# k weights in three row chunks, x tile 1 behind b1 on the scalar queue, filler matmuls between the first transposes, last tile stored in two column parts

## Chip, cores, metric

One core of a Trainium2 chip. The metric is the device time of one execution in microseconds (us). Most executions of one kernel agree within a few tenths of a us; where a run is more than 1.5% above the fastest of the same kernel it is called slow and is not compared. The profile's engines are PE (matmul), PEld (weight load), DVE, ACT, POOL and SP; "q" behind a name means the engine's sequencer, which issues DMAs.

## The reference, cut to what matters

```python
x = A_x                               # (1, 2048, 448), bfloat16
xn = _layernorm(x, axis=-1)
s = _A_ref(xn, A_wqkv, A_wo)          # linear attention, 16 heads of 28, feature map elu-like
g = _silu(_B_ref(xn, B_w1, B_b1, B_w2, B_b2))   # squared-relu MLP, hidden size 1792
return x + s * g
```

Everything begins with the layer norm of x. x is 16 tiles of 128 tokens; "x tile 1" is the second one. "k" are the attention's keys, b1 is the first bias of the MLP, and H is the MLP's hidden layer. Its first four blocks are computed in two halves: the first for the tokens of tiles 0 and 1, the second for those of tiles 2 and 3. When the second halves start, the slow start of the kernel is over.

## The kernel before

The program writes a list of operations, a small scheduler in Python orders them, and each engine gets a fixed instruction stream. The parts that the change touches are the first loads, the first PE operations, and the last store.

```python
# first loads: x tile 0 and the weights on the SP queue, x tiles 1, 2-3 and b1 on the ACT (scalar) queue
load_x(0, 1)
load_x(1, 2, "act").prio = -118
load_k("sp", w_qkv, A_wqkv, "wk", 384, 2 * D)      # one 384 KB transfer + two of 64 KB
load_x(2, 4, "act").prio = -117
dma("act", b1r[0:NF, :], B_b1..., ["b1r"], F * 2, ["b1r"]).prio = -115
load_w1("w1a", 0, 512, 2)
load_x(4, 8)
# ... cut

# the head of PE's stream
warm(10, wide=True)          # ten 128x512 matmuls on a constant, to have the PE clock released
# ... cut
turn(0, 0, "act")            # PE transposes of normalised x tile 0, tile 1 (PSUM -> xT by ACT or DVE)
turn(0, 1, "act")
turn(1, 0, "act")
mains(k0, (0, 1), [("xT", 0, 0)] + wnames("wk")[:1])
turn(1, 1, "dve")
# ... cut

# DVE's and ACT's order in the head is pinned: each op comes after those before it in the list
("dve", "st0 mv0 st1 mv1 xn00 xn01 xd0 xn10 xn11 xd1 st2 mv2 xT11 st3 mv3 xn2 xd2 xn3 xd3 xT3"),
("act", "ln0 ex0 ln1 ex1 xT00 xT01 xT10 ln2 ex2 b1 ln3 ex3 xT2"),
```

`st` and `mv` are the statistics of a tile, `ln`/`ex` make the reciprocal deviation, `xn` normalises, `xd` copies the last 64 columns, `xT` copies a transpose out of PSUM. `st1`, which needs x tile 1, stands second in DVE's order. Each engine works its stream in order.

## Time and profile before

| | before |
|---|---|
| median of 6 runs | 142.26 us (142.20 to 142.73) |
| span in the profile | 141.2 us |
| PE busy | 98% |
| DVE's statistics of tiles 0 and 1 start | 3.40, 4.16 us |
| dense PE work starts (second halves of H) | 10.18 us |
| last store: issue to landing | 139.45 to 141.17 = 1.72 us |

The page of the kernel before, its first lines and the chain of work that ended last, by engine:

```profile
span 141.2 us, 3056 instructions
...
PE 98%; DVE 0%; issue 0%; DVEq 0%
```

So time changes only if PE's dense stretch starts sooner or later, if holes come into it, or if the tail after it changes. The head is seen in the timeline of DVE, kernel before (start, length, engine, line, operation, output<-input, and in brackets the idle time before it with what ended it):

```profile
3.40 0.63 DVE L451 BATCH_NORM_STATS2 st<-x_tok 128x6 f32<-128x448 bf16 x1 [3.40 <-DMA x_tok<-in_A_x_dram]
4.06 0.18 DVE L452 BATCH_NORM_AGGREGATE mv<-st 128x2 f32<-128x6 f32 x1
4.16 0.59 DVE L451 BATCH_NORM_STATS2 st<-x_tok 128x6 f32<-128x448 bf16 x1
4.79 0.18 DVE L452 BATCH_NORM_AGGREGATE mv<-st 128x2 f32<-128x6 f32 x1
4.89 0.56 DVE L474 TENSOR_SCALAR xn<-x_tok,mv,rstd 128x256 bf16<-128x256 bf16 x2
...
6.28 0.62 DVE L451 BATCH_NORM_STATS2 st<-x_tok 128x6 f32<-128x448 bf16 x1
...
9.73 0.42 DVE L513 COPY xT<-pb 128x512 bf16<-128x512 bf16 x1 [0.32 <-PE pb L503]
```

DVE waits once, for x tile 0, and then runs almost without a pause until the last transpose copy. The second line of statistics (4.16) has no bracket: tile 1 was there already; the trace's semaphore records have it landed at 3.57. PE's dense stretch starts at 10.18, right behind that last copy (PE timeline, kernel before):

```profile
5.26 1.10 PE L503 MATMUL pb<-ident,xn 128*128 128x128 bf16 x6
...
10.18 1.91 PE L661 MATMUL pb<-xT,w 64*128 64x256 bf16 x32
```

The ACT queue's first DMAs, kernel before: x tiles 1 and 2-3, then b1.

```profile
0.83 0.89 ACTq L396 DMA_DIRECT2D x_tok<-in_A_x_dram  x2
1.76 0.70 ACTq L396 DMA_DIRECT2D b1r<-in_B_b_dram  x1
```

### The profile page before, as it was taken

The page shows a single profiled execution, that of the slowest core. Times are in us where ns is not written, and L with a number is a line of the kernel's source. Part 1 is how long each engine was busy: PE and PEld are TensorE (multiplying, and loading weights), DVE is VectorE, ACT ScalarE, POOL GpSimd, SP SyncE. Part 2 cuts the span into 40 slices and gives each one's busy share as a digit, 9 for nine tenths or more (in the row PEclk, how much of TensorE's full clock was granted, in tenths as well). Part 3 has the DMA queues.
Part 4 walks back from the last instruction along what each step waited for, and adds up shares of the span by engine and source line. Part 5 has one row for each costly group of instructions (what it writes and reads, how often), then busy time and mean ns, then how long its engine had stood idle before and what let it go on. Part 6 is the DMA issues. An engine that isn't in the chain of part 4 may idle for free.

```text
span 141.2 us, 3056 instructions
## 1 busy us (share of the span) xinstructions
PE 137.8 (98%) x1225; PEld 68.4 (48%) x1225; DVE 92.0 (65%) x224; ACT 78.7 (56%) x152; POOL 22.9 (16%) x38
## 2 busy tenths in 40 slices
PE   7999999999999999999999999999999999999992
PEld 2366444444444444444445445654555555555482
DVE  0989978898878998779959910127936062452743
ACT  3558787987888897879799571333033030300220
POOL 6000000000000000000680000000001419092670
DMA  4997266999713400000000025880000202122032
GB/s 111 310 312 235 50 170 97 366 300 210 137 23 74 84 14 0 0 9 14 0 0 0 5 76 151 200 155 14 5 0 0 68 2 89 41 66 69 33 102 67
DMA packets 20210, 12.91 MB, mean 91 GB/s; under 512 B 9380, under 2 KB 19812, under 8 KB 20196
## 3 DMA queue, kind: packets, MB, share of 16 engines
q1 hardware_dynamic: 18044, 11.22, 32.1%
q10 hardware_dynamic: 2152, 1.50, 4.4%
q8 instruction: 10, 0.16, 0.5%
q14 instruction: 4, 0.03, 0.1%
HBM read 8.78 MB, written 2.10 MB: 77 GB/s over the span
## 4 chain that ended last, share of the span: by engine, by line
PE 98%; DVE 0%; issue 0%; DVEq 0%
PE pb L928 30%; PE pb L661 30%; PE pb L614 9%; PE pb L994 8%; PE pb L695 7%; PE pb L645 6%; PE pb L1035 3%; PE pb L503 1%; PE pb L701 1%; PE pb L788 1%; PE pb L749 1%; PE pb L826 0%; DVE xn L964 0%; PE pb L819 0%; DVE xn L973 0%; PE pb L784 0%
## 5 line engine op out<-in xcount | busy, mean ns | idle before, releaser
L661 PE MATMUL pb<-xT,w 64*128 64x512 bf16 (+2 forms) x408 | 51.3, 365 | 0.0
L928 PE MATMUL pb<-w,r 64*128 64x448 bf16 (+3 forms) x378 | 44.7, 343 | 0.0
L670 ACT ACTIVATE r<-pb,b1f 128x512 bf16<-128x512 f32 x56 | 35.0, 690 | 2.8 <-PE pb L661 2.8
L661 PEld LDWEIGHTS pb<-xT,w 64*128 64x128 bf16 (+1 forms) x408 | 22.8, 94 | 22.1 <-ACT r L670 0.5
L928 PEld LDWEIGHTS pb<-w,r 64*128 64x128 bf16 (+1 forms) x378 | 22.8, 95 | 20.0 <-issue 1.2
L904 ACT ACTIVATE gbuf<-gbuf 128x448 bf16<-128x448 bf16 (+1 forms) x16 | 8.6, 564 | 36.4 <-DVE gbuf L939 34.3
L939 DVE TENSOR_TENSOR gbuf<-pb,b2b 128x448 bf16<-128x448 f32 (+1 forms) x16 | 9.3, 608 | 29.3 <-PE pb L928 29.3
L973 POOL TENSOR_TENSOR xn<-xn,x_tok 128x448 bf16<-128x448 bf16 x15 | 15.0, 1030 | 48.8 <-DVE xn L964 48.8
L614 PE MATMUL pb<-w_qkv,xT 64*128 64x512 bf16 (+1 forms) x106 | 17.9, 379 | 0.0
L645 PE MATMUL pb<-xT,w_qkv 64*128 64x512 bf16 x84 | 15.5, 376 | 0.0
L678 DVE TENSOR_TENSOR r<-r 128x512 bf16<-128x512 bf16 x39 | 13.5, 416 | 0.0
L385 POOL MEMSET kvm<- 128x2048 bf16 x1 | 1.8, 1804 | 64.4 <-DVE zb L639 64.4
L451 DVE BATCH_NORM_STATS2 st<-x_tok 128x6 f32<-128x448 bf16 x16 | 9.3, 611 | 3.4 <-DMA x_tok<-in_A_x_dram 3.4
L592 ACT ACTIVATE qk<-pb 128x512 bf16<-128x512 f32 x16 | 8.9, 594 | 4.1 <-PE pb L614 3.6
L602 DVE SCALAR_TENSOR_TENSOR qk<-pb,qk 128x512 bf16<-128x512 f32 x16 | 10.7, 686 | 0.3
L994 PE MATMUL pb<-msb,pqT 64*128 64x448 bf16 (+3 forms) x93 | 10.9, 343 | 0.0
L964 DVE TENSOR_TENSOR xn<-pb,gbuf 128x448 bf16<-128x448 f32 (+2 forms) x17 | 9.2, 590 | 2.0 <-ACT gbuf L904 1.5
L679 ACT ACTIVATE r<-r 128x512 bf16<-128x512 bf16 x17 | 9.7, 651 | 0.0
L614 PEld LDWEIGHTS pb<-w_qkv,xT 64*128 64x128 bf16 (+1 forms) x106 | 6.7, 95 | 6.2 <-DVE xT L513 0.2
L695 PE MATMUL pb<-qk,xn 128*128 128x448 bf16 x48 | 9.4, 352 | 0.0
L592 ACT ACTIVATE pqT<-pb 128x512 bf16<-128x512 f32 x12 | 6.8, 597 | 3.1 <-PE pb L661 1.6
L645 PEld LDWEIGHTS pb<-xT,w_qkv 64*128 64x128 bf16 x84 | 6.0, 94 | 5.0
(77 smaller groups left out, 98.9 us busy)
## 6 DMA issues: line engine op xcount, KB each, us to landing
out_dram<-xn SPq DMA_DIRECT2D x15, 112.0 KB, 1.7
w<-in_B_w_dram SPq DMA_DIRECT2D x1, 1568.0 KB, 9.8
x_tok<-in_A_x_dram SPq DMA_DIRECT2D x3, 448.0 KB, 3.8
xT<-rows ACTq DMA_DIRECT2D x6, 112.0 KB
w<-in_B_w_dram SPq DMA_DIRECT2D x1, 576.0 KB, 5.7
xT<-rows SPq DMA_DIRECT2D x5, 112.0 KB
w_o<-in_A_wo_dram SPq DMA_DIRECT2D x1, 392.0 KB, 11.0
w_qkv<-in_A_wqkv_dram SPq DMA_DIRECT2D x1, 384.0 KB, 4.7
```

The lines of the kernel that those rows point to most:

```text
L592: add("act", lambda e, _: e.activation(out=slot, in_=src(), func=AF.Exp), [buf, "actw"], [tile], 0.6)
L602: lambda e, _: e.scalar_tensor_tensor(out=slot, in0=src(), scalar=1.0 + 1e-6, in1=slot, op0=ALU.add, op1=ALU.max),
L614: return e.matmul(ps(b)[:, 0:512], xT[half[h], c, si * P : (si + 1) * P], w_qkv[half[h], c, 384 : 2 * D], start=start, stop=stop,)
L645: return e.matmul(ps(b)[:, 0:512], w_qkv[half[h], c, m * P : (m + 1) * P], xT[half[h], c, g * 512 : (g + 1) * 512], start=start, stop=stop,)
L661: return e.matmul(ps(b)[:, c0 : c0 + n], w_1[half[h], c, fi * P : (fi + 1) * P], xT[half[h], c, t : t + n], start=start, stop=stop,)
L670: lambda e, _: e.activation(out=slot, in_=ps(b)[:, 0:512], func=AF.Relu, bias=b1f[:, fi : fi + 1]),
L678: return e.tensor_tensor(out=slot, in0=slot, in1=slot, op=ALU.mult)
L679: return e.activation(out=slot, in_=slot, func=AF.Square)
L695: last = e.matmul(ps(b)[:, 0:D], xn[:, si, c * P : (c + 1) * P], pk_of(si), start=(si == 0), stop=(si == NT - 1),)
L928: return e.matmul(ps(b)[:, 0:n], r2[half[h], fi, si * P : (si + 1) * P], w_2[half[h], fi, c], start=start, stop=stop)
L973: eng, lambda e, _: e.tensor_tensor(out=ob, in0=ob, in1=x_tok[:, si, c], op=ALU.add),
L994: return e.matmul(ps(b)[:, 0:n], q, m, start=start, stop=stop)
```

## The change

Its intent: let the first k matmul begin on the first chunk of weights; leave the memory to x tile 0 and the weights first; have PE busy in the holes between the first transposes, so that its clock is released; and shorten the final store.

```diff
-load_x(1, 2, "act").prio = -118
-load_k("sp", w_qkv, A_wqkv, "wk", 384, 2 * D)
-load_x(2, 4, "act").prio = -117
-dma("act", b1r[0:NF, :], B_b1..., ["b1r"], F * 2, ["b1r"]).prio = -115
+dma("act", b1r[0:NF, :], B_b1..., ["b1r"], F * 2, ["b1r"]).prio = -118
+load_x(1, 2, "act").prio = -117
+for c in range(3):
+    dma("sp", w_qkv[:, c, 384 : 2 * D], A_wqkv[c * P : (c + 1) * P, 384 : 2 * D],
+        [("wk", (0, 3, 4)[c])], P * 1024)
+load_x(2, 4, "act").prio = -116
+for i in (0, 1):
+    dma("sp", w_qkv[half[i], 3, 384 : 2 * D], A_wqkv[384:448, 384 : 2 * D], [("wk", 1 + i)], 64 * 1024)
 ...
 turn(0, 1, "act")
+warm(3)
 turn(1, 0, "act")
-mains(k0, (0, 1), [("xT", 0, 0)] + wnames("wk")[:1])
+warm(2)
+mains(k0, (0,), [("xT", 0, 0), ("wk", 0)])
+mains(k0, (1,), [("wk", 3)])
 turn(1, 1, "dve")
 ...
 full(ss(15, ca, eng="dve", end=False), KS, ["msz"])
+store(15, ca)                       # columns 0-255, SP queue
 full(gg(15, cb, True), range(NF + 1))
 full(ss(15, cb, eng="dve", end=False), KS, ["msz"])
-store(15, [ca, cb], "act")          # 448 columns
+store(15, cb, "act")                # columns 256-447
```

## The prediction

> What bounds it now. The page's chain of waits is 98% PE, and the windows view has PE busy all the time from 10.2 to 138.5 us. So the change can only move the start of the dense stretch and the tail after it.
>
> The head is paced by a DVE chain, not by PE. In the timeline of the first 12 us, x tile 0 lands at 3.40 (it was issued at 0.81), and from there DVE runs almost without a pause, in a fixed order: statistics of tile 0 (0.63), of tile 1 (starts 4.16), normalise tile 0 (4.89, 5.17), tile 1 (5.57) and so on, to the last transpose copy at 9.73-10.15. The second halves of H, where dense PE work begins, start at 10.18.
>
> Step 1, three row chunks. The first K matmul starts at 6.16. By the semaphore records of the trace the big k load had landed at 5.99, while the ACT copy of tile 0's transpose ended at 6.07. So chunks take away a wait that was already hidden: 0 to 0.1 us. They cost two more issues on SP, about 0.5 us each; later loads are issued about 1 us later, but they queue for bandwidth (311-369 GB/s from 3 us) and landed over 4 us after issue, so little of that should show.
>
> Step 2, x tile 1 behind b1. The b1 issue holds the ACT queue for 0.70 us and waits for a memset ending at 1.00, so x tile 1 is issued near 1.75 instead of 0.83. Tile 0 loses its competitor and should land 0.2-0.3 us earlier, near 3.15. Tile 1, which landed at 3.57 with 0.6 us to spare, should land at 3.9-4.4 (2.2-2.6 us after issue, estimated from tile 0's 2.6). DVE needs it second, so the chain moves by -0.2 to +0.25 us. The Trainium skill ("DMA: Bandwidth & Descriptors", anatomy of one DMA) gives a fixed part of about 2 us per transfer; here 112 KB took 1.7 us in the stores and 2.6 in the first load.
>
> Step 3, five small matmuls of 128 columns. Cold they cost 0.107 us each, warm 0.055. The trace shows PE cold through the first K matmul (the second, at 6.58, is mostly fast). The Trainium skill ("TensorE: Matmul & The Clock Gate", part 1) says the gate watches a free-running window of about 3.4 us; the idle bits between 5.07 and 6.16 sum to about 0.5 us. Filling them makes the release surer, but the three runs before differ by only 0.17 us, so it was hardly missed. If the clock is still cold, the fillers push the first K matmul and the second transpose of tile 1 back, up to 0.2 us on the DVE chain; if warm, nothing. Expected +0.05.
>
> Step 4, last store in two parts. Now the chain ends: residual ends 139.42, issue 139.45, landed 141.17: 1.72 us, of which the packets of 112 KB took about 0.5. With 48 KB on this path about half of that goes: -0.15 to -0.25 us, perhaps less since a row is then 384 B.
>
> Sum: head about 0 (-0.2 to +0.45), tail -0.2, on 142.2: 142.0 us. Within 2% almost surely.
>
> Right or wrong in the profile: the last store's issue to landing under 1.6 us; DVE's first statistics near 3.15 and its second one waiting for the load of x tile 1; the first K matmul no earlier than 6.0; start of the 256-column second H halves at 10.0 to 10.5; PE solid after that.
>
> What would make it wrong: w1 loads arriving after PE wants them (8 and 12 us), because SP issues later; a clock gate that stays cold one more window; a different order picked by the scheduler in the middle.

## The result

The changed kernel takes 142.75 us (median of 6, 142.58 to 143.26), the kernel before 142.26. The ratio is 1.0036 with a 95% interval of 1.0015 to 1.0057: slower by half a us. The prediction said 142.0, at most 142.45. A ratio here is the mean time of one kernel's fast runs over that of the other's of the same rounds, so not quite the ratio of the medians.

| | before | changed |
|---|---|---|
| x tile 0 landed | 3.38 | 2.84 |
| x tile 1 issued, landed | 0.83, 3.57 | 1.70, 4.53 |
| statistics of tile 1 start | 4.16 | 4.55 |
| second halves of H start | 10.18 | 10.45 |
| last store issued | 139.45 | 139.72 |
| last store, issue to landing | 1.72 | 1.58 |

(Landings are the last of the 16 semaphore increments of the transfer in the trace.) From the second halves of H to the last store's issue both take the same 129.27 us: 139.45 - 10.18 and 139.72 - 10.45. The middle is out of it, and so it is, within 0.01 us, in the profiles of e1, e3, e4, e5, e6, e9, e15 and e17 below.

The page of the changed kernel, first line and chain by engine:

```profile
span 141.4 us, 3071 instructions
...
PE 94%; DMA 2%; DVE 1%; ACT 1%; issue 0%; DVEq 0%
```

A load has come into the chain. Which one, the chain in order of time says (changed kernel, first 12 us; start, length, what):

```profile
0.80 0.87 ACT L428
1.67 0.04 issue
1.70 2.82 DMA x_tok<-in_A_x_dram
4.53 0.02 issue
4.55 0.64 DVE st L458
```

It is x tile 1. DVE's timeline of the changed kernel answers the one above:

```profile
2.86 0.63 DVE L458 BATCH_NORM_STATS2 st<-x_tok 128x6 f32<-128x448 bf16 x1 [2.86 <-DMA x_tok<-in_A_x_dram]
3.52 0.18 DVE L459 BATCH_NORM_AGGREGATE mv<-st 128x2 f32<-128x6 f32 x1
4.55 0.63 DVE L458 BATCH_NORM_STATS2 st<-x_tok 128x6 f32<-128x448 bf16 x1 [0.85 <-DMA x_tok<-in_A_x_dram]
5.21 0.18 DVE L459 BATCH_NORM_AGGREGATE mv<-st 128x2 f32<-128x6 f32 x1
5.31 0.55 DVE L481 TENSOR_SCALAR xn<-x_tok,mv,rstd 128x256 bf16<-128x256 bf16 x2
...
6.70 0.62 DVE L458 BATCH_NORM_STATS2 st<-x_tok 128x6 f32<-128x448 bf16 x1
...
10.00 0.42 DVE L520 COPY xT<-pb 128x512 bf16<-128x512 bf16 x1 [0.32 <-PE pb L510]
```

The first statistics start 0.54 us sooner, and all of it is lost: DVE idles 0.85 us in front of the second ones, in order, because they stand second in its stream. Everything behind them is 0.4 us later at first, 0.27 at the end of the head. The same lateness is seen on PE, which now idles before its first transposes (the bracket) and starts the dense stretch at 10.45 (changed kernel):

```profile
5.68 0.69 PE L510 MATMUL pb<-ident,xn 128*128 128x128 bf16 x4 [0.42 <-DVE xn L481]
...
10.45 1.91 PE L667 MATMUL pb<-xT,w 64*128 64x256 bf16 x32
```

and what delays the tile in the ACT queue (changed kernel), where b1's issue holds x tile 1 back until 1.70:

```profile
1.03 0.64 ACTq L397 DMA_DIRECT2D b1r<-in_B_b_dram  x1
1.70 0.87 ACTq L397 DMA_DIRECT2D x_tok<-in_A_x_dram  x2
```

The last store is one more line, from the list of DMA issues (output<-input, issuer, count, KB each, us to landing), kernel before:

```profile
out_dram<-xn ACTq DMA_DIRECT2D x1, 112.0 KB, 1.7
```

and changed kernel:

```profile
out_dram<-xn ACTq DMA_DIRECT2D x1, 48.0 KB, 1.6
```

The pair of profiles explains only +0.27 - 0.14 = +0.13 us of the half us. Much of the rest is in the choice of the runs: the changed kernel's profiled run (142.68) was one of its quicker ones, while that of the kernel before took 142.46, 0.20 above its median, with its first k matmul still at half clock (shown under e3). With the first k matmuls at full speed in both, as in the changed profile, the old order has its second halves at 9.95 to 10.02 (e1, e10, e17), which is 0.43 to 0.50 us before the 10.45 of the change.

### The profile page after: what moved, and what is told of

The parts are those of the page before. It is cut to its first block, busy times and chain, and to the rows that moved or that the text cites. A ratio compares the mean times of both kernels' runs of the same rounds, so it can differ in the third digit from the quotient of the medians.

```text
span 141.4 us, 3071 instructions
## 1 busy us (share of the span) xinstructions
PE 137.7 (97%) x1230; PEld 68.6 (49%) x1230; DVE 92.0 (65%) x224; ACT 78.6 (56%) x152; POOL 22.9 (16%) x38
## 4 chain that ended last, share of the span: by engine, by line
PE 94%; DMA 2%; DVE 1%; ACT 1%; issue 0%; DVEq 0%
PE pb L934 30%; PE pb L667 30%; PE pb L620 9%; PE pb L1000 8%; PE pb L701 7%; PE pb L651 6%; DMA x_tok<-in_A_x_dram 2%; PE pb L510 1%; PE pb L707 1%; PE pb L794 1%; ACT L428 1%; PE pb L755 1%; PE pb L832 0%; DVE st L458 0%; DVE xn L970 0%; PE pb L825 0%
```

## The experiments

Three theories were tried against each other. A: x tile 1 lands late and DVE's in-order stream waits. B: the fillers push the k matmuls back, or the two extra issues on SP delay the weights. C, formed after the first four runs: the late tile opens a hole in PE's work in front of the first transposes, and the PE clock, which starts at half speed (the first wide warm-up matmuls of both profiles start 0.43 us apart, full-speed ones 0.22), is then released later or taken back.

Each call ran up to four kernels on one chip, with their own runs of the kernel before; the four calls were on four chips. Means are of fast runs.

| run | edit | median (range of fast runs) | ratio to before (95%) | statistics of tile 1 start | second halves of H start |
|---|---|---|---|---|---|
| e1 | changed, old ACT order | 142.16 (142.15-142.27) | 0.9983 (0.9963-1.0003) | 4.12 | 9.99 |
| e2 | before, new ACT order alone | 145.01 (143.66-145.33) | 1.0167 (1.0134-1.0201) | 5.29 | 12.47 |
| e3 | changed, no fillers | 143.37 (142.66-144.55) | 1.0072 (1.0030-1.0115) | 4.82 | 11.99 |
| e4 | before, cut store alone | 142.56 (142.35-142.73) | 1.0008 (0.9987-1.0029) | 4.17 | 10.04 |
| e5 | before, fillers alone | 142.35 (142.25-143.65) | 1.0011 (0.9977-1.0044) | 4.17 | 10.24 |
| e6 | e2, 13 wide warm-up matmuls | 143.62 (143.24-143.99) | 1.0083 (1.0061-1.0105) | 5.48 | 11.38 |
| e7 | changed, k in one piece | 144.99, all six (143.62-145.00) | 1.0139 (1.0101-1.0177) | profile slow | profile slow |
| e8 | changed, x tile 1 second on SP | 142.60 (142.27-143.41) | 1.0018 (0.9991-1.0045) | 3.80 | 9.73 |
| e9 | changed, 12 wide warm-up matmuls | 142.80 (142.70-142.99) | 1.0028 (1.0015-1.0041) | 4.21 | 10.64 |

### e1_order_undone: the change with the old order on the ACT queue

```diff
-b1 (prio -118); x tile 1 (-117); x tiles 2-3 (-116)      # ACT queue of the changed kernel
+x tile 1 (-118); x tiles 2-3 (-117); b1 (-115)           # as before
```

> The changed kernel with the scalar queue's old order (x tile 1, x tiles 2-3, b1); all else of the change kept. Theory A (x tile 1 lands at 4.53 instead of 3.57 us and the DVE chain waits for it): x tile 1 lands near 3.6, DVE's second statistics no longer wait, second H halves start near 10.1-10.2 (10.45 after), and the time is 142.0 us, 0.5 to 0.9 below the changed kernel, a little under the kernel before. Theory B (the five filler matmuls, or the two extra issues on SP, are the cost): still 142.6 to 142.9.

142.16, with a spread of 0.12 us. DVE's second statistics no longer wait (timeline of e1, no bracket):

```profile
3.36 0.63 DVE L458 BATCH_NORM_STATS2 st<-x_tok 128x6 f32<-128x448 bf16 x1 [3.36 <-DMA x_tok<-in_A_x_dram]
4.02 0.18 DVE L459 BATCH_NORM_AGGREGATE mv<-st 128x2 f32<-128x6 f32 x1
4.12 0.59 DVE L458 BATCH_NORM_STATS2 st<-x_tok 128x6 f32<-128x448 bf16 x1
```

The dense stretch starts at 9.99 (PE timeline of e1):

```profile
9.99 1.91 PE L667 MATMUL pb<-xT,w 64*128 64x256 bf16 x32
```

Theory A passes. Chunks, fillers and cut store, all of which are still in, cost nothing here: B falls.

### e2_order_alone: the new order put into the kernel before

```diff
-x tile 1; x tiles 2-3; b1      # ACT queue of the kernel before
+b1; x tile 1; x tiles 2-3
```

> The kernel before with only the scalar queue's order changed (b1, x tile 1, x tiles 2-3). Theory A: x tile 1 lands at 4.3-4.6, second statistics wait for it, and the time is 142.7 to 143.0, i.e. 0.4 to 0.7 above before, with a wider spread from run to run than before. Theory B: 142.2 to 142.3 as before.

145.01: the loss is four times what A forecast, so A alone is not enough. Two things are new. First, x tile 1 landed at 5.26 (4.53 in the changed kernel), so the statistics started 5.29 - 4.16 = 1.13 us late. Second, the clock. The windows view of e2 (window, its length, busy time of PE, PEld, DVE, ACT, POOL with instructions, then the granted PE clock, DMA share, GB/s):

```profile
5.00:6.00 1.00, 0.00 (x0) 0.00 (x0) 0.68 (x2) 0.00 (x0) 0.00 (x0) 1.00 1.10 264
6.00:7.00 1.00, 0.58 (x4) 0.30 (x4) 0.97 (x6) 0.75 (x3) 0.00 (x0) 1.00 1.18 279
7.00:8.00 1.00, 0.97 (x7) 0.52 (x7) 0.96 (x4) 0.82 (x3) 0.00 (x0) 0.78 1.15 312
8.00:9.00 1.00, 1.00 (x6) 0.45 (x4) 0.96 (x4) 0.50 (x2) 0.00 (x0) 0.50 1.00 370
9.00:10.00 1.00, 1.00 (x5) 0.43 (x4) 0.73 (x4) 0.00 (x0) 0.00 (x0) 0.50 1.10 341
10.00:11.00 1.00, 1.00 (x7) 0.71 (x5) 0.29 (x1) 0.57 (x3) 0.00 (x0) 0.51 1.11 303
```

PE does nothing from 5 to 6 us; from about 7.56 (0.78 = 1 - 0.44/2) to 10.98 the clock is granted at one half, for 3.4 us. The Trainium skill ("TensorE: Matmul & The Clock Gate", part 1) describes a free-running window of about 3.4 us that sets the clock by PE's activity; the length agrees. The other runs of e2 fit: the four with a mean granted clock of 0.988 took 144.84 to 145.33, the one with 0.999 took 143.66 (one with 0.998 took 145.11). This gave theory C.

### e3_no_fill: the change without the five fillers

```diff
-warm(3)
-warm(2)
```

> The changed kernel without the five filler matmuls. Theory A: as the changed kernel, 142.6 to 142.9, or up to 0.2 slower if the fillers help the clock. Theory B, fillers: 142.3 or less.

143.37, in two groups: three runs at 142.66 to 142.87, three at 143.87 to 144.55. The profiled run (144.13, fast by the rule) is of the upper group. PE by operation and shape, first 13 us (busy us, mean ns of one) in e3:

```profile
L620 PE MATMUL pb<-w_qkv,xT 128*128 128x512 bf16 x6 | 3.0, 634 | 0.0
```

against the kernel before and the changed kernel:

```profile
L614 PE MATMUL pb<-w_qkv,xT 128*128 128x512 bf16 x6 | 1.8, 429 | 0.0
```

```profile
L620 PE MATMUL pb<-w_qkv,xT 128*128 128x512 bf16 x6 | 1.6, 378 | 0.0
```

In e2 such a matmul takes 634 ns where the clock column shows 0.50 and 379 where it shows 1.00. So a mean of 634 ns means that all six first k matmuls ran at half speed, 378 that none did; in the kernel before one was slow and one was caught in the change. (Initial half speed is not in the trace's clock column, which shows 1.00 there; the matmul lengths have to be read.) The transposes of tiles 2 and 3 wait behind these matmuls in PE's order, and the dense stretch starts at 11.99. The clock column of e3 shows the release at 9.98. If the windows are 3.41 us long, as in e2, the one before ended at 6.57 (an estimate), nearly when the kernel before got its clock (during its second k matmul, which starts at 6.58). There PE had no hole in front of the first transposes; here it had one of 0.69 us, and the clock was not released. One profile against another is little, but it is what theory C says.

B, which had the fillers as a cost, falls again. That they are a gain is not shown: 143.47 - 142.85 = 0.6 us on the mean comes from different calls, and rests on three runs of six in the upper group. The changed kernel, with fillers, has one such run in thirteen: the profiled run of e16 below (144.59, slow). There the tile landed at 4.87, the hole was 0.76 us, the clock came at 10.02, and the first k matmuls took up to 631 ns in spite of the fillers, which started at 6.56. Fillers cannot fill the hole in front of the first transposes, as they stand behind four of these in PE's stream.

### e4_tail_alone: the kernel before with the cut store

```diff
-store(15, [ca, cb], "act")
+store(15, ca)            # after ss(15, ca)
+store(15, cb, "act")
```

> The kernel before with only the last store cut in two column parts. Last store's issue to landing 1.59 instead of 1.72 us, so 142.1, 0.10 to 0.15 below before, whichever theory holds. If it is slower than before, the smaller rows or the extra wait at the end cost something the trace of the changed kernel doesn't show.

142.56, ratio 1.0008: no gain. In its profile the last store took 1.98 us, not 1.59: fifteen of the sixteen increments were there after 1.64 us and the last came 0.34 later. Over all fast profiles the store in one piece took 1.72 or 1.73 in each of seven, the cut one 1.58, 1.59, 1.59, 1.60, 1.60, 1.67, 1.70, 1.72 and 1.98 (mean 1.67). The gain exists in five of these nine; in the other four the last increment came 0.10 to 0.34 us behind the fifteenth and ate most or all of it. The timed comparison is below, under e17.

### e5_fill_alone: the kernel before with the fillers

```diff
+warm(3)    # after turn(0, 1)
+warm(2)    # after turn(1, 0)
```

> The kernel before with only the five filler matmuls. Theory C (the clock gate needs a window with PE busy; the late tile opens a hole of 0.4 to 1.6 us in front of the first transposes, which can cost a whole further window of about 3.4 us at half speed): before has only a small hole (0.2 us), so fillers gain little: 142.2 to 142.3, without the stray slow runs of 142.5 to 143.1 that the kernel before shows. Theory B (fillers push the K matmuls back): 142.4 or more.

142.35, ratio 1.0011: no gain seen, though the interval (about -0.3 to +0.6 us) is wide. The hope that stray slow runs would go failed: one run was 143.65.

### e6_order_gap_filled: the new order with a longer warm-up

```diff
 # e2, and:
-warm(10, wide=True)
+warm(13, wide=True)
```

> The kernel before with the scalar queue's new order and 13 instead of 10 wide warm-up matmuls, which fill the hole in front of the first transposes. Theory C: the clock no longer goes or stays slow, and only the delay of the DVE chain remains, about 0.5 to 1.1 us as the load lands at 4.6 to 5.3: 142.8 to 143.4, over 1.5 us below the order alone (145.0), trace clock 1.0 after its release. Rival (the order's 2.7 us are all chain delay or late weights): 144.5 to 145.3.

143.62, 1.4 us below e2, and the mean granted clock is 0.999 or 1.0 in all six runs. The hole was not filled, only made shorter. The first transposes with the idle time before them, in e2 and then in e6:

```profile
6.42 1.00 PE L503 MATMUL pb<-ident,xn 128*128 128x128 bf16 x6 [1.64 <-DVE xn L474]
```

```profile
6.61 1.00 PE L503 MATMUL pb<-ident,xn 128*128 128x128 bf16 x6 [1.28 <-DVE xn L474]
```

The time is a little more than forecast, since the tile landed at 5.45, later than the range it was forecast from. What is left is 0.83% of 142.4 = 1.2 us, and in the profile the second halves start 11.38 - 10.18 = 1.2 us late. So e2's loss splits in two: 1.2 us of waiting for the tile, and the other half of its 1.67% (2.4 us) for the clock. The rival, all waiting, expected 144.5 or more and falls.

### e7_chunks_undone: the change with the k weights in one piece

```diff
-for c in range(3): dma("sp", w_qkv[:, c, 384 : 2 * D], ...)
+load_k("sp", w_qkv, A_wqkv, "wk", 384, 2 * D)
```

> The changed kernel with the k weights loaded in one piece again (order, fillers, tail of the change kept). In the traces so far x tile 1 landed at 4.53 and 4.79 with chunks and at 5.26 without, so if the chunks are what lets the late tile land sooner: x tile 1 lands near 5.2, time 143.3 to 144.8, well above the changed kernel's 142.75. If chunks don't matter: 142.6 to 142.9.

144.99, or 144.40 as the mean of its four fast runs, against 142.85 with chunks. The fast profiles with the new order have x tile 1 landed at 4.53, 4.79 and 4.18 with chunks (changed, e3, e9) and at 5.26 and 5.45 without (e2, e6). So the chunks do matter in the new order, though not by what they were meant for: they let the late tile land about 0.8 us sooner. The packet records of these five traces tell where the time goes. The tile is issued at 1.70 or 1.71 in all of them, but its first packet moves at 2.84, 2.88 and 2.91 with chunks and at 3.77 and 3.75 without; by then 282 and 268 of the 384 packets of the k piece had started on SP's queue (87 to 106 k packets with chunks). From there on the two go side by side: in the changed kernel the scalar queue and SP's queue moved about 180 and 220 KB from 2.75 to 4.25 us. The Trainium skill ("DMA: Bandwidth & Descriptors", queues, rings and completion order) says an engine takes the queues in turn, a packet at a time; that fits the second stretch. It does not account for the first, and what holds the tile's packets back behind a long transfer was not shown.

### e8_x1_on_sp: x tile 1 second on SP's queue

```diff
-load_x(1, 2, "act").prio = -117
+load_x(1, 2)                        # SP, behind x tile 0, ahead of the k chunks
```

> The changed kernel with x tile 1 as the second transfer of the SP queue, ahead of the k chunks; b1 stays first on the scalar queue. Tile 0 should land near 2.85 as in the changed kernel, tile 1 at 3.3 to 3.7, so that DVE's second statistics start near 3.6 to 3.75 instead of 4.16 (before) or 4.55 (changed). If nothing else binds, 141.7 to 141.9, below both; if tiles 2-3 or the w1 load bind in turn, about 142.0 to 142.2.

The head did what was wanted: statistics of tile 1 at 3.80, second halves at 9.73, 0.45 us ahead of the kernel before. Yet the time was 142.60. The gain went in a new wait, as DVE's timeline of e8 shows:

```profile
9.28 0.42 DVE L520 COPY xT<-pb 128x512 bf16<-128x512 bf16 x1 [0.33 <-PE pb L510]
10.55 1.15 DVE L458 BATCH_NORM_STATS2 st<-x_tok 128x6 f32<-128x448 bf16 x2 [0.84 <-DMA x_tok<-in_A_x_dram]
11.62 0.48 DVE L601 TENSOR_SCALAR qk<-qk 128x512 bf16<-128x512 bf16 x2
```

x tiles 4-7 are issued on SP behind three more transfers than before (6.73 against 5.31) and landed at 10.53 against 9.23. DVE waits for them in order, the feature map of the first two K tiles stands behind them, and PE has a hole of 0.41 us at 12.76, ended by that feature map, and another of 0.48 us at 25.34, for which the profile names no wait. (Holes are counted here from one matmul's start to the next one's, less the usual 0.2 us; the profile's own idle times, 0.25 and 0.32, are shorter.) Together they are the 0.93 us by which the stretch to the last store is longer than 129.27.

### e9_after_gap_filled: the change with two more wide warm-up matmuls

```diff
-warm(10, wide=True)
+warm(12, wide=True)
```

> The changed kernel with 12 instead of 10 wide warm-up matmuls, which fill the hole of about 0.4 to 0.6 us that its late x tile 1 leaves in front of the first transposes. Theory C (late tile = delay of the DVE chain, plus a clock release that some runs get late): the slow runs of the changed kernel (143.1, 143.3) go, the low ones stay: 142.6 to 142.8 with a spread under 0.3 us. If the spread stays, it comes from the landing time of the tile itself.

142.80, with 0.29 us from lowest to highest where the changed kernel had 0.68 and e16, below, 0.79. The slow runs go, as expected, but so do the lowest (142.58 there and 142.41 in e16; here 142.70), and the mean is the same, 142.82 against 142.85. It is no cure. In its profile the tile landed at 4.18, early enough, but the clock was still at half speed and the warm-up itself ran until about 5.9, so the transposes could not start before 5.91.

### e10, e11, e12: chunks and fillers with one store, and x tile 1 on SP with k in one piece

```diff
 # e10: e1, last store in one piece
 # e11: kernel before + b1 first on ACT, x tile 1 second on SP, fillers
 # e12: e11 + cut last store
```

> The changed kernel with the old order on the scalar queue and the last store in one piece: chunks and fillers alone. Beside the run with the cut store (142.16, ratio to before 0.9983): if the cut saves the 0.13 us seen between the traces, 142.25 to 142.35; if stragglers of the smaller packets eat it, 142.1 to 142.2. Against the fillers alone (142.3) it shows what the chunks do in the old order: 0 to -0.1.

> The kernel before with b1 first on the scalar queue, x tile 1 second on SP, the five fillers; k weights in one piece and the last store in one piece. With x tile 1 on SP and chunks the head was 0.45 us shorter, but x tiles 4-7 landed at 10.53, DVE waited 0.84 for them and PE lost 0.9 later. With two issues fewer on SP, tiles 4-7 should land at 9.3 to 9.8, no such wait, and the head gain should stay: 141.8 to 142.0. If the stalls stay: 142.5 as with chunks.

> As the run before it in this call, but the last store cut in two as in the change. 0.10 to 0.15 us below it if the cut is worth what the trace of the changed kernel shows; equal within 0.05 or slower if the last packets straggle as in the store-alone run.

e10: 142.64 (142.30 to 143.54), ratio 1.0026 (0.9999 to 1.0053), above its forecast. It has a faster head than before (9.95) and in its profiled run, the slowest, two PE holes of 0.61 and 0.67 us at 25.25 and 99.42. The next call ran the same file again at 142.30, so these are not a property of the kernel. e11: 143.20, ratio 1.0054; e12: 143.32, ratio 1.0059. Both failed: with the k weights in one piece x tiles 4-7 landed later still (11.01 and 11.77), and PE had a hole of 0.70 and 0.89 us behind them. In e12 the k weights were late too: the first k matmul, after 0.82 us of idleness, started at 6.73, behind their landing at 6.60. e12 against e11 says nothing of the store; the spread is larger than the effect.

### e13, e15, e16, e17: one chip for the decisive comparison

```diff
 # e13: e8, and in DVE's order the feature map of K tiles 0, 1 ahead of the statistics of tiles 4, 5
-op.after = [head["xT3"]]
+op.after = [head["xT3"]] + [o for o in early if o.eng == "dve"]
 # e15: e1 again      # e16: the changed kernel again      # e17: e10 again
```

> The changed kernel with x tile 1 second on SP (as in the run that had a head 0.45 us shorter and lost 0.9 us in two later PE stalls), and with the K feature-map work of tiles 0 and 1 put ahead of the statistics of tiles 4 and 5 in DVE's order. If the first stall came from DVE waiting in order for x tiles 4-7, no PE gap near 12.8 us remains and the time is 141.7 to 142.1. If the late loads bind by themselves, the stall only moves: 142.3 to 142.8.

> The changed kernel with the scalar queue's old order, once more, on one chip with the changed kernel itself and the one-store version. Theory A/C: 142.1 to 142.3 and 0.4 to 0.6 below the changed kernel on the same chip. If its 142.16 was a kind chip: 142.4 to 142.7.

> The changed kernel itself, once more: 142.6 to 143.2, mean 142.85; x tile 1 lands at 4.2 to 4.8 and the second H halves start at 10.4 to 10.6.

> Old order on the scalar queue, chunks and fillers, last store in one piece, once more. If the cut of the last store is worth its 0.13 us: 0.10 to 0.15 above the order-undone run of this call. If it is worth nothing on the mean: equal within 0.05. If this version again shows 142.6 with stray runs over 143 while the other stays tight, the difference lies in something else than the store.

| run | median | mean of fast runs | ratio to before (95%) |
|---|---|---|---|
| e13 x tile 1 on SP, feature map first | 142.46 | 142.62 | 1.0005 (0.9973-1.0037) |
| e15 change, old ACT order | 142.36 | 142.38 | 0.9988 (0.9960-1.0015) |
| e16 change | 142.99 | 142.90 | 1.0023 (0.9990-1.0056) |
| e17 change, old ACT order, one store | 142.30 | 142.33 | 0.9985 (0.9957-1.0012) |

e16 against e15: 142.90 - 142.38 = 0.52 us for the order of three DMAs on one queue, all else equal; five of the six fast runs of e16 lie above every run of e15. That is the size of the whole loss in the first comparison (142.85 - 142.34 on the means). Against the kernel before of this call, which had stray runs up to 143.38, the loss is only 0.36 us and not clear of noise. e16's profiled execution was slow, so no difference is explained by it. e17 against e15: the cut store is worth nothing, 0.05 us on the wrong side. e13: the hole near 12.8 us is gone, as expected if DVE's order made it, but smaller ones of 0.2 us came at 14.70 and 39.94, and with stray runs at 142.87 and 143.23 it does not beat the kernel before. Its forecast of 141.7 to 142.1 missed.

No version beat both kernels beyond doubt. e1, e15 and e17 are the best; their intervals just include 1.

## Why the prediction was wrong, point by point

- **What bounds the kernel**: right. 129.27 us from the second halves of H to the last store's issue, before and after, and the loss lies ahead of it.
- **Step 1, chunks "take away a wait that was already hidden: 0 to 0.1 us"**: right in the old order, as far as the runs go (e15 and e17, which hold chunks, are within 0.2% of before). Wrong as a statement about the change: in the new order the chunks set when x tile 1 lands, and without them the change costs some 1.5 us more (e7, 144.40 against 142.85). Parts of a change were costed one at a time, and these two are not independent.
- **Step 2, "Tile 1 ... should land at 3.9-4.4 ... so the chain moves by -0.2 to +0.25 us"**: this is the step that failed. Mechanism and direction were named; the size was not. The tile landed at 4.53, 2.83 us after its issue, not 2.2-2.6: tile 0's 2.57 before, from which the estimate came, was measured in the other order of the queues. In the fast profiles of kernels with chunks it landed at 4.18 to 4.79. The chain moved by +0.39 at the second statistics, by 0.43 to 0.50 at the second halves of H (10.45 against 9.95 to 10.02 in e10, e1 and e17, with the first k matmuls at full speed in all), and by 0.52 in time (e16 against e15). That the profile's 10.45 lies inside the predicted 10.0 to 10.5 is partly luck: the 10.18 it was reckoned from belongs to a run 0.20 us above its median. Tile 0 landed 0.54 sooner, more than the 0.2-0.3 predicted, and was worth nothing, as DVE's second operation waits for tile 1 and all of tile 0's work stands behind it.
- **Step 3, fillers, "+0.05"**: too small a question was asked. It priced the fillers in the old order, where no effect of theirs is seen (e5). It did not see that the late tile of step 2 opens a hole in PE's work in front of the first transposes (0.42 us in the changed profile, 0.69 in e3, 1.64 in e2), with which the clock can come a window later (e3) or be taken back (e2). The fillers stand behind that hole, and whether they mend what it does is not shown. The statement "hardly missed", read from three runs of the kernel before, was carried over to a kernel in which the release was no longer sure.
- **Step 4, last store "-0.15 to -0.25 us"**: the profile shows -0.14. Timed, no gain is seen (e15 against e17; e4). The sum counted a best case.
- **Sum**: "head about 0, tail -0.2". Measured: 0.5 slower. The late tile and what it brings cost 0.52 by e16 against e15; the other parts together gain little (e15 and e17 at ratios of 0.9988 and 0.9985, intervals including 1). How the 0.52 splits in the changed kernel between waiting and clock is not measured directly. Its profiled run, clock released early, has the dense stretch at 10.45 against 9.95 to 10.41 in the four profiles of the old order with chunks and fillers (e1, e10, e15, e17; 10.41 was one with the clock released late). To the other three, whose first k matmuls ran at full speed as the changed profile's did, it is 0.43 to 0.50 us, so waiting is most of it. The stray slow runs of several kernels, the one before included, stay unexplained.

## What to carry to other kernels

Here an engine that works its stream in order was held by the second load it needs, not the first: before moving a load back, look at which instruction of each stream needs it, and how much slack the semaphore records give (here 0.6 us, against 0.9 of later issue and a busier memory). A late load that leaves PE idle in its first microseconds can cost as much through the clock as through the wait itself (1.2 us each in e2), so look at the lengths of the first matmuls too. Cost the parts of a change together: the chunks here were worth next to nothing in the old order and some 1.5 us once another part had made the tile late. And before two profiles are subtracted, see where each of the two runs lies among the runs of its kernel.

## What the Trainium skill lacked or had wrong

- "TensorE: Matmul & The Clock Gate", part 1 and its closing table, warns of single PE-idle gaps of about 3 us and more. In e2 a gap of 1.64 us, with only short transposes and two k matmuls behind it, was enough: the clock went to one half for 3.4 us. In e6, with a longer warm-up ahead of it, one of 1.28 us was not. The page does not say how busy a window has to be; its part 4 says that transposes don't count as busy in the same way, which fits but was not tested here.
- The same page says the release varies by when the window falls. Runs agree: in the eight fast profiles of other runs whose clock column shows a release it came at 3.94 to 6.12, and in e3 at 9.98. e3's six runs fall into 142.66-142.87 and 143.87-144.55, which may be its price in a thinly filled head (only one of them was profiled).
- "DMA: Bandwidth & Descriptors", anatomy of one DMA, gives about 2 us fixed per transfer (for the gpsimd path). Here the 112 KB final store on the scalar queue took 1.72-1.73 us in all seven fast profiles, and x tile 0, issued first and without x tile 1 beside it, 2.04 in the changed kernel. The page's table of specifications says that pieces under 512 B are read, modified and written; it does not tell of scatter. The 48 KB store in 384 B rows took 1.58 to 1.98 us, and no run here tests whether the row size is the reason.
- No page gives a number for how a short load fares next to a long one on the other queue. Here the same 112 KB, issued at 1.70, moved its first packet at 2.84-2.91 and landed at 4.18-4.79 beside 128 KB pieces; beside a 384 KB one these were 3.75-3.77 and 5.26-5.45.
